# Operand addresses modulo 256: x, g and the sums moved by some tens of bytes in a pooled-attention and FFN kernel

## The chip, the core and the metric

The kernel runs on one NeuronCore of a Trainium2 chip; the other seven cores are idle. The metric is the device time of one execution in microseconds (us). The engines are named as in the profile: PE is TensorE (its weight loads, which overlap the matmuls, are PEld), DVE is VectorE, ACT is ScalarE, POOL is GpSimd, SP is the queue that issues the DMAs. Each engine runs its own instructions in order and waits on semaphores for the others. TensorE multiplies a *stationary* operand, loaded as weights, with a *streamed* operand that passes through it column by column. Both lie in SBUF, the on-chip memory of 128 partitions, where a tile is a range of bytes that has the same address in each partition. The text speaks of addresses *modulo 256*: the remainder of a tile's first byte when divided by 256.

## The reference

The inputs are q, k, v of shape 8 × 8 × 576 × 64 and the weights w_in (512 × 2048) and w_out (2048 × 512), all float32.

```python
k_p = k.reshape(B, H, Sp, 8, D).mean(axis=3)      # 576 keys pooled to 72
v_p = v.reshape(B, H, Sp, 8, D).mean(axis=3)
scores = scale * q @ k_p.T;  scores -= scores.max(-1)
attn = exp(scores) / (sum(exp(scores)) + 1e-9)
x = (attn @ v_p)  as 4608 tokens x 512
h = x @ w_in
g = max(h, 0) + log1p(exp(-abs(h)))               # softplus
out = g @ w_out                                    # 4608 x 512
```

## The kernel before

The 4,608 tokens are cut into 18 chunks of 256 (`CT`). Each chunk goes through attention, which leaves x for it, and then through the two products of the feed-forward part. The second axis of the weights is cut into 16 pieces of 128 (`FC`), treated in 8 pairs u (`FP`).

Each float32 operand of the large products is carried as a rounded high part and a low part, the remainder. A product is then three matmuls: high by high, high by low, low by high. In the first product (`ffn1_products`, L488) a 128 × 128 piece of w_in is stationary and 256 columns of x stream past it; a chunk has 16 × 4 × 3 = 192 such matmuls. Softplus on ACT gives g, a second activation its rounded part gh, and DVE the low part gl.

The second product exists in two forms. In the first four chunks (`ffn2`, L510, and `pair2`, L570) a 128-token piece of g is stationary and 512 columns of w_out stream. In the other fourteen (`pair2_fast`, L678) seven products of half width take the place of eight: sums and differences of g's quarters (`sums`, L588 to L591), rounded on ACT into `so` (L602) with a low part from DVE (L607), are stationary beside gh and gl, and 256 columns of w_out or of combined weights stream past them. That is 21 matmuls for each pair u.

The weights stay in SBUF: 16 tiles of 8,192 bytes per partition, in the pool `wpool`. All that comes and goes lies in the pool `one`: the loads (L, X4 to X6), q (A4), the pooled keys and values, the transposed q (G4, G5), the row minima mn and row sums sm of the softmax (two buffers of 32 bytes each), the exponentials E, the buffers G0 to G3, o0 and o1 for g, the sums and the outputs, pe for the normalized last eight columns, pT and Y for the transposed probabilities, X01 and X23 for x, and Sa and Sb for `so`. The x of the third chunk lies in Sa and Sb, before these hold sums.

Modulo 256 the kernel before has them so, with p for the place of the weights: q, the loads and qT at p; the minima and sums between p and p + 96; E at p + 32; buffer G3 at p + 128; everything behind pe (pT, x, the other buffers of g, gh, gl, so, the outputs) at p − 64. The tile pe has 192 floats in use and 16 more that nothing reads, 832 bytes in all.

The order of the work is computed ahead by a planner (`Order`): each operation has an engine, an estimated cost and its predecessors, and the planner lists them by rank and by hand-set offsets (`HASTE`). It knows slots (names of buffers), but no addresses. The program then issues every operation in that order, on all of ACT, DVE, PE and SP.

Of the kernel before, what the change touches and what calls it, by code (L numbers as in the profile page):

```python
# [9 lines left out]
F32 = mybir.dt.float32  # L10
F32R = mybir.dt.float32r
# [92 lines left out]
def pooled_attention_softplus_ffn(  # L104
# [11 lines left out]
    B, H, S, D = q.shape  # L116
    NTOK, DM = out.shape
    DFF = w_in.shape[1]
    P = 128
# [5 lines left out]
    CT = T * P  # L125
    HP = H // 2
# [3 lines left out]
    N1 = 3  # L130
# [5 lines left out]
    PSUM = bass.MemoryType.PSUM  # L136
    const = ctx.enter_context(tc.tile_pool(name="const", bufs=1))
    wpool = ctx.enter_context(tc.tile_pool(name="wpool", bufs=1))
    one = ctx.enter_context(tc.tile_pool(name="one", bufs=1))
    psum = ctx.enter_context(tc.tile_pool(name="psum", bufs=1, space=PSUM))  # L140
    dram = ctx.enter_context(tc.tile_pool(name="dram", bufs=1, space=bass.MemoryType.DRAM))
# [149 lines left out]
    R = 4 * KL  # L291
# [19 lines left out]
    def new_x(c, name=None):  # L311

        if c == N1 - 1:
            x_[c] = [one.tile([P, HP, CT], F32R, tag=tag, name="x") for tag in ("Sa", "Sb")]
        else:
            x = one.tile([P, 2, HP, CT], F32R, tag={"a": "X01", "b": "X23"}[name or "ab"[c % N1]],
                         name="x")
            x_[c] = [x[:, 0], x[:, 1]]

# [3 lines left out]
    class Tile:  # L323
# [30 lines left out]
        def least(self, j, ps, tag):  # L354

            if j == 0:
                self.mn = one.tile([P, 2, HP], F32, tag="mn" + tag, name="mn")
            nc.vector.tensor_reduce(out=self.mn[:, j], in_=self.view(ps), axis=AX.X, op=ALU.min)  # L358

        def view(self, ps):  # L360
# [9 lines left out]

        def exp_sum(self, j, ps, tag):
            if j == 0:
                self.sm = one.tile([P, H], F32, tag="sm" + tag, name="sm")
            for m in range(HP):
                h = 4 * (m // 2) + 2 * j + m % 2
                nc.scalar.activation(out=e_[self.c][:, self.t, h], in_=self.view(ps)[:, m],  # L376
                                     func=AF.Exp, scale=-1.0, bias=self.mn[:, j, m:m + 1],
                                     accum_out=self.sm[:, h:h + 1])

        def sum(self, tag):  # L380
            self.sm = one.tile([P, H], F32, tag="sm" + tag, name="sm")
            nc.vector.tensor_reduce(out=self.sm, in_=e_[self.c][:, self.t], axis=AX.X, op=ALU.add)

        def reciprocal(self):
# [7 lines left out]
                                    in1=self.sm.unsqueeze(2).to_broadcast([P, H, KM]), op=ALU.mult)  # L392

        def ends(self):

            pe = one.tile([P, 6 * R + 16], F32, tag="pe", name="pe")
            self.pe = pe[:, 0:6 * R].rearrange("p (a n r) -> p a n r", a=2, n=3)
            for a in range(2):
                hs = slice(4 * a, 4 * a + 4)
                nc.vector.tensor_tensor(  # L400
                    out=self.pe[:, a].rearrange("p n (h j) -> p n h j", h=4),
                    in0=e_[self.c][:, self.t, hs, KM:SP].unsqueeze(1).to_broadcast([P, 3, 4, KL]),
                    in1=self.sm[:, hs].unsqueeze(1).unsqueeze(3).to_broadcast([P, 3, 4, KL]),
                    op=ALU.mult)
# [61 lines left out]
    def av_high(c, r, ps, name=None):  # L466
        if c not in x_:
            new_x(c, name)
        nc.scalar.copy(out=x_[c][0][:, r::2], in_=ps.rearrange("p (g i) -> p g i", g=2))
# [475 lines left out]
    def attend(c):  # L945
# [17 lines left out]
        for t, x in enumerate(tiles):  # L963
# [7 lines left out]
            q_free[c, t] = o  # L971
            o = op(ACT, act(512), lambda x=x, s=s_q, n=s_qT: x.qT_out(s.tile, n.name), [o], [s_q, s_qT])
            ends, ss = [], [Slot("bank"), Slot("bank")]
            p = op(PE, 0.7, lambda x=x, ss=ss: x.scores([bank(s, "sc") for s in ss]), [o, *keys],
                   [s_qT, *ss])
            score_done.setdefault(c, []).append(p)
            for i, s in enumerate(ss):
                d = op(DVE, 0.46, lambda x=x, i=i, s=s, n=s_mn: x.least(i, s.tile, n.name), [p, *ends],
                       [s, s_mn])
                if c < N1:  # L980
                    def exp_sum(x=x, i=i, s=s, e=s_E[0], t=t, n=s_sm):
                        if c == 0 and 0 not in e_:
                            new_E(0)
                        e_[c] = e_[0]
                        x.slot = e.name
                        x.exp_sum(i, s.tile, n.name)
                    ends.append(op(ACT, 1.2, exp_sum, [d], [s, s_mn, s_sm, *s_E], table="exp"))
                else:
                    def less(x=x, i=i, s=s):
                        if c not in e_:  # L990
                            new_E(c)
                        x.less(i, s.tile)
                    ends.append(op(DVE, 0.46, less, [d, *e_free], [s, s_mn]))
            if c < N1:
                exps.extend(ends)
            else:
                subs += ends
            norms.append((x, ends, s_E, s_sm, s_pm, s_pe))
        if c == N1:
            ex = op(ACT, 1.2, lambda: exponential(e_[c]), subs, table="exp")  # L1000
# [403 lines left out]
```

## Time and profile before

| | us |
|---|---|
| two runs | 903.52 and 904.15, median 903.84 |
| the profiled execution | 903.13 |
| its span on the core | 901.4 |
| PE busy | 883.9 (98%) |
| PEld busy | 840.9 (93%) |
| DVE busy | 648.7 (72%) |
| ACT busy | 407.5 (45%) |
| DMA queue q1 | 189.82 MB, 68.2% of 16 engines |

A group of the profile names line, engine and operation, the output and its inputs by the program's names, the shape, the count, busy time in us and the mean of one in ns, and the engine's idle time ahead of them with what ended it. Matmuls overlap in the pipeline: one lasts some 280 ns from its start to its end, but the next starts far earlier, so their throughput is read from the distance between starts. The timeline merges equal neighbours into one row with the start of the first, the time to the end of the last, and the count. The chain is the sequence of work that ended last, followed back from the last instruction. In the rows by windows stand, for each engine, busy time and number of instructions, then the granted clock, the share of the DMA engines and GB/s.

### The profile page before, as it was taken

Reading aid. Unit: us, or ns where it says so; the run is one execution under the profiler, and the core shown is the slowest. Engines: PE = TensorE matmul, PEld = TensorE weight load, DVE = VectorE, ACT = ScalarE, POOL = GpSimd, SP = SyncE. Lnnn points to the kernel's source line nnn. Section 1 sums busy time; section 2 is a strip of 40 time slices with the busy share of each in tenths; the row PEclk is TensorE's granted clock in tenths of the full one; section 3 lists DMA queues with packets and bytes.
Section 4 is the critical chain, followed back from the end, with each engine's and each line's share of the span. In section 5 each row is a group of like instructions: output and inputs, shape, how many; then the busy total and the mean of one; then the engine's idle time right before and its main releaser. Section 6 shows DMA issues by size and latency. Waiting matters only on the chain.

```text
span 901.4 us, 20496 instructions
## 1 busy us (share of the span) xinstructions
PE 883.9 (98%) x8304; PEld 840.9 (93%) x8304; DVE 648.7 (72%) x1600; ACT 407.5 (45%) x824; POOL 2.4 (0%) x19
## 2 busy tenths in 40 slices
PE   5999999999999999999999999999999999999997
PEld 3689999889999999999999999999999999999997
DVE  5899999878767678787767666776576565657454
ACT  5864443354353534443444444353545353434332
POOL 1000000000000000000000000000000000000000
PEclk9999999999999999999999999999999999999999
DMA  9976544545997788787669765877566565656472
GB/s 233 312 227 202 173 162 158 161 153 200 299 267 240 231 239 245 214 249 228 227 200 261 217 227 168 257 239 228 193 179 228 177 222 187 212 162 225 163 241 76
DMA packets 107085, 191.12 MB, mean 212 GB/s; under 512 B 46064, under 2 KB 60400, under 8 KB 106992
## 3 DMA queue, kind: packets, MB, share of 16 engines
q1 hardware_dynamic: 106992, 189.82, 68.2%
q8 instruction: 65, 1.06, 0.5%
q14 instruction: 28, 0.23, 0.1%
HBM read 167.25 MB, written 22.54 MB: 211 GB/s over the span
## 4 chain that ended last, share of the span: by engine, by line
PE 95%; DVE 2%; DMA 1%; SPq 1%; ACT 1%; issue 0%; DVEq 0%; ACTq 0%
PE h L488 44%; PE m L678 31%; PE acc L510 7%; PE acc L570 3%; PE sc L351 2%; PE avp L455 2%; PE qTp L331 2%; PE ptp L414 2%; PE avp L462 1%; DMA wst<-in_moe_w_out_dram 1%; PE ltp L426 1%; DMA kvl<-in_v_dram 1%; ACT E L376 0%; SPq L302 0%; DVE o L699 0%
## 5 line engine op out<-in xcount | busy, mean ns | idle before, releaser
L488 PE MATMUL h<-x,w 128*128 128x256 f32 x3456 | 428.7, 280 | 0.2 <-ACT g L493 0.2
L488 PEld LDWEIGHTS h<-x,w 128*128 128x128 f32 x3456 | 413.3, 188 | 4.2 <-ACT g L493 0.6
L537 ACT ACTIVATE g<-h 128x512 f32<-128x512 f32 x120 | 71.9, 599 | 280.3 <-PE h L488 277.7
L678 PE MATMUL m<-w,so 128*128 128x256 f32 x1344 | 173.9, 278 | 0.0
L678 PEld LDWEIGHTS m<-w,so 128*128 128x128 f32 x1344 | 163.8, 188 | 0.0
L678 PE MATMUL m<-w,gh 128*128 128x256 f32 x672 | 131.6, 285 | 0.0
L588 DVE TENSOR_TENSOR sf<-g 128x128 f32<-128x128 f32 x112 | 32.7, 292 | 130.1 <-ACT g L537 129.6
L678 PEld LDWEIGHTS m<-w,gh 128*128 128x128 f32 x672 | 102.1, 188 | 1.7
L602 ACT CAST so<-sf 128x512 fp32r<-128x512 f32 x112 | 69.7, 622 | 58.1 <-DVE sf L591 57.6
L607 DVE TENSOR_TENSOR so<-sf,so 128x512 fp32r<-128x512 f32 x112 | 77.3, 690 | 22.8 <-ACT so L602 22.7
L678 PE MATMUL m<-w,gl 128*128 128x256 f32 x336 | 93.5, 278 | 0.0
L558 DVE TENSOR_TENSOR gl<-g,gh 128x384 fp32r<-128x384 f32 (+1 forms) x120 | 67.2, 560 | 0.5 <-ACT gh L551 0.3
L678 PEld LDWEIGHTS m<-w,gl 128*128 128x128 f32 x336 | 63.0, 188 | 0.0
L510 PE MATMUL acc<-w,g 128*128 128x512 f32 x192 | 60.1, 394 | 0.0
L551 ACT ACTIVATE gh<-h 128x384 fp32r<-128x384 f32 (+1 forms) x120 | 59.2, 493 | 0.0
L493 ACT ACTIVATE g<-h 128x256 fp32r<-128x256 f32 x96 | 32.1, 383 | 56.6 <-PE h L488 34.3
L699 DVE TENSOR_TENSOR o<-o,m 128x256 f32<-128x256 f32 x98 | 39.7, 417 | 3.5 <-ACT o L691 0.6
L510 PEld LDWEIGHTS acc<-w,g 128*128 128x128 f32 x192 | 33.5, 188 | 5.2
L510 PE MATMUL acc<-w,gl 128*128 128x512 f32 x96 | 37.9, 395 | 0.2 <-DVE gl L499 0.2
L591 DVE TENSOR_TENSOR sf<-g,sf 128x128 f32<-128x128 f32 x112 | 32.7, 292 | 3.9
L358 DVE TENSOR_REDUCE mn<-sc 128x4 f32<-128x288 f32 x72 | 31.3, 450 | 5.5 <-PE sc L351 5.4
L400 DVE TENSOR_TENSOR pe<-E,sm 128x96 f32<-128x96 f32 x72 | 15.2, 252 | 27.7 <-PE ltp L426 27.7
(165 smaller groups left out, 925.8 us busy)
## 6 DMA issues: line engine op xcount, KB each, us to landing
w<-wi SPq DMA_DIRECT2D x224, 512.0 KB
out_dram<-o SPq DMA_DIRECT2D x36, 256.0 KB
q<-in_q_dram SPq DMA_DIRECT2D x32, 256.0 KB
wst<-in_moe_w_in_dram SPq DMA_DIRECT2D x32, 256.0 KB
wst<-in_moe_w_out_dram SPq DMA_DIRECT2D x16, 512.0 KB
wi<-w SPq DMA_DIRECT2D x16, 512.0 KB
kst<-in_k_dram SPq DMA_DIRECT2D x24, 288.0 KB
vst<-in_v_dram SPq DMA_DIRECT2D x24, 256.0 KB
```

What stands on the lines that cost most here:

```text
L488: nc.tensor.matmul(out=ps[:, 0:CT], lhsT=row(w, kc), rhs=x[:, kc], start=first and kc == j == 0, stop=last and kc == KC - 1 and j == 2)
L493: nc.scalar.activation(out=g, in_=ps[:, 0:CT], func=AF.Softplus)
L510: nc.tensor.matmul(out=accs[c][t], lhsT=a[:, ts], rhs=w, start=f == 0 and j == 0, stop=f == FC - 1 and j == 2)
L537: nc.scalar.activation(out=g, in_=x.rearrange("p (b i) -> p b i", i=P), func=AF.Softplus)
L551: nc.scalar.activation(out=gh, in_=quarters(c, x.rearrange("p (b i) -> p b i", i=P)), func=AF.Softplus)
L558: nc.vector.tensor_tensor(out=gl, in0=quarters(c, g), in1=gh.bitcast(F32), op=ALU.subtract)
L588: tt(out=sf[:, 2], in0=g[:, 0], in1=g[:, 2], op=ALU.add)
L591: tt(out=sf[:, 3], in0=g[:, 3], in1=sf[:, 1], op=ALU.subtract)
L602: nc.scalar.copy(out=so[:, 0], in_=ss[c, u])
L607: nc.vector.tensor_tensor(out=so[:, 1], in0=sf, in1=so[:, 0].bitcast(F32), op=ALU.subtract)
L678: nc.tensor.matmul(out=ms[c][n], lhsT=x, rhs=y, start=u == 0 and j == 0 and n in (1, 6, 5, 4), stop=u == FP - 1 and j == 2 and n in (2, 7, ...
L699: nc.vector.tensor_tensor(out=o, in0=in0, in1=m[n], op=how)
```

## The change

The tiles of x for all chunks but the third leave the big pool for one of their own, which opens behind an unused tile of 32 bytes; the minima and sums get a small pool with an unused tile of 64 bytes; and pe loses its 16 unused floats. Operations, their order, their shapes and the number of buffers stay.

```diff
     wpool = ctx.enter_context(tc.tile_pool(name="wpool", bufs=1))
+    room = ctx.enter_context(tc.tile_pool(name="room", bufs=1))
+    room.tile([P, 8], F32, name="room")
+    xpool = ctx.enter_context(tc.tile_pool(name="xpool", bufs=1))
+    mpool = ctx.enter_context(tc.tile_pool(name="mpool", bufs=1))
+    mpool.tile([P, 16], F32, name="room")
     one = ctx.enter_context(tc.tile_pool(name="one", bufs=1))
...
-            x = one.tile([P, 2, HP, CT], F32R, tag={"a": "X01", "b": "X23"}[name or "ab"[c % N1]],
+            x = xpool.tile([P, 2, HP, CT], F32R, tag={"a": "X01", "b": "X23"}[name or "ab"[c % N1]],
                          name="x")
...
-                self.mn = one.tile([P, 2, HP], F32, tag="mn" + tag, name="mn")
+                self.mn = mpool.tile([P, 2, HP], F32, tag="mn" + tag, name="mn")
...
-                self.sm = one.tile([P, H], F32, tag="sm" + tag, name="sm")
+                self.sm = mpool.tile([P, H], F32, tag="sm" + tag, name="sm")
...
         def sum(self, tag):
-            self.sm = one.tile([P, H], F32, tag="sm" + tag, name="sm")
+            self.sm = mpool.tile([P, H], F32, tag="sm" + tag, name="sm")
...
         def ends(self):
-
-            pe = one.tile([P, 6 * R + 16], F32, tag="pe", name="pe")
-            self.pe = pe[:, 0:6 * R].rearrange("p (a n r) -> p a n r", a=2, n=3)
+            self.pe = one.tile([P, 2, 3, R], F32, tag="pe", name="pe")
```

## The prediction

> **What bounds the kernel now.** I read the page's engine table and chain first, to see which engine sets the end and with which lines; then the groups of its two large lines; then the timeline of TensorE alone in the middle of the run, because the change alters no instruction and can only act through how long one of them takes.
>
> ```profile
> span 901.4 us, 20496 instructions
> ...
> PE 883.9 (98%) x8304; PEld 840.9 (93%) x8304; DVE 648.7 (72%) x1600; ACT 407.5 (45%) x824; POOL 2.4 (0%) x19
> ...
> PEclk9999999999999999999999999999999999999999
> ...
> PE 95%; DVE 2%; DMA 1%; SPq 1%; ACT 1%; issue 0%; DVEq 0%; ACTq 0%
> PE h L488 44%; PE m L678 31%; PE acc L510 7%; PE acc L570 3%; PE sc L351 2%; PE avp L455 2%; PE qTp L331 2%; PE ptp L414 2%; PE avp L462 1%; DMA wst<-in_moe_w_out_dram 1%; PE ltp L426 1%; DMA kvl<-in_v_dram 1%; ACT E L376 0%; SPq L302 0%; DVE o L699 0%
> ```
>
> TensorE is 98% busy at full clock and is 95% of the chain. Nothing off TensorE can give back more than a few per cent, and 75% of the chain is two lines: L488 (the first product, x streams past a stationary piece of w) and L678 (the fast second product, w streams past a stationary piece of g or of a sum).
>
> ```profile
> L488 PE MATMUL h<-x,w 128*128 128x256 f32 x3456 | 428.7, 280 | 0.2 <-ACT g L493 0.2
> ...
> L678 PE MATMUL m<-w,so 128*128 128x256 f32 x1344 | 173.9, 278 | 0.0
> ...
> L678 PE MATMUL m<-w,gh 128*128 128x256 f32 x672 | 131.6, 285 | 0.0
> ...
> L678 PE MATMUL m<-w,gl 128*128 128x256 f32 x336 | 93.5, 278 | 0.0
> ```
>
> That is 3,456 of L488 and 1,344 + 672 + 336 = 2,352 of L678, 5,808 matmuls of one shape. Their idle time is nil, so what counts is how far apart they start. The timeline merges equal neighbours (start, time from first start to last end, count), and it shows two speeds for the same work:
>
> ```profile
> 489.52 2.90 PE L488 MATMUL h<-x,w 128*128 128x256 f32 x24
> ...
> 492.94 1.52 PE L678 MATMUL m<-w,so 128*128 128x256 f32 x12
> 494.30 0.39 PE L678 MATMUL m<-w,gh 128*128 128x256 f32 x2
> 494.52 0.28 PE L678 MATMUL m<-w,gl 128*128 128x256 f32 x1
> 494.64 2.99 PE L488 MATMUL h<-x,w 128*128 128x256 f32 x24
> ...
> 498.18 1.57 PE L678 MATMUL m<-w,so 128*128 128x256 f32 x12
> 499.59 0.40 PE L678 MATMUL m<-w,gh 128*128 128x256 f32 x2
> 499.83 0.28 PE L678 MATMUL m<-w,gl 128*128 128x256 f32 x1
> 499.94 0.60 PE L414 MATMUL ptp<-ident,pm 128*128 128x128 f32 x4
> ```
>
> One matmul alone lasts 0.28 us, so twelve that take 1.52 start (1.52 − 0.28)/11 = 113 ns apart, and twelve that take 1.57 start 117 ns apart. Counted by starts the two spacings are 113.3 and 117.8 ns, and hardly anything lies between them: a group falls into one and stays in it to its end. Engine, shape, clock and operands' places modulo 256 are the same in both. The pass of 45 matmuls from 489.52 to 494.64 takes 5.12 us, the next, from 494.64 to 499.94, takes 5.30. So the kernel alternates between a fast and a slow gait, and which one it has depends on how it started, not on which data it reads.
>
> How often each? Of the 112 groups of twelve on the sums, 110 stand unbroken in the timeline; 47 take 1.52 and 63 take 1.57 to 1.61. First and last of them:
>
> ```profile
> 244.60 1.52 PE L678 MATMUL m<-w,so 128*128 128x256 f32 x12
> ...
> 894.65 1.61 PE L678 MATMUL m<-w,so 128*128 128x256 f32 x12
> ```
>
> So 57% of L678 is slow. For L488 the length of a group also holds a wait at its start, so I counted the starts themselves: of its 3,366 spacings between 112 and 130 ns, 1,600 are 116 or more (48%), mean 115.59. For L678 there are 2,303 such spacings, mean 115.94.
>
> **The change, by its addresses.** Let p be the weights' place modulo 256 (all 16 weight tiles are 8,192 B, so they share it). Before, the tiles ahead of x and g in the big pool are multiples of 256 B except two minima and two sums of 32 B and pe, which is 832 B = 3×256 + 64. So x, g, gh, gl, so stand at p + 4×32 + 64 = p − 64 modulo 256 (the buffer G3, ahead of pe, at p + 128). After, room (32 B) puts x at p + 32; the two x tiles are 8,192 B each, the small pool holds 64 + 4×32 = 192 B, so the big pool begins at p + 32 + 192 = p − 32, and as pe is now 768 B, all of it stands there. In terms of what TensorE reads, the streamed operand against the stationary one: L488 goes from −64 to +32, L678, L510 and L570 from +64 to +32. The x of the third chunk lies in the sums' buffers, so the 192 matmuls of L488 that read it go to −32.
>
> No instruction, wait, queue or transfer is added, removed or moved; the order on each engine comes from a planner that knows no addresses. Net space is +32 B. So the sum has one kind of term: so many matmuls by the change of their spacing.
>
> *Why the place can matter at all.* The streamed operand covers 256×4 = 1,024 B of each partition per matmul, the weights loaded meanwhile for the next 128×4 = 512 B. Modulo 256 the first laps the second twice per matmul. If a meeting costs some 4.5 ns, one meeting and two give two spacings 4.5 ns apart, as seen. Where both operands are 128 wide there is nothing to lap, and the transposes bear that out:
>
> ```profile
> L414 PEld LDWEIGHTS ptp<-ident,pm x144: 138/140/144, 22.2 to 834.2; 128*128 128x128 f32 x144
> L414 PE MATMUL ptp<-ident,pm x144: 270/272/328, 22.3 to 834.3; 128*128 128x128 f32 x144
> ```
>
> Four of them take 0.60 us (row above), so they start (0.60 − 0.27)/3 = 110 ns apart (109 by starts), as pm lies at either of two places. By this reading 109 is no meeting, 113.3 one, 117.8 two. It is an inference, not a row.
>
> *What +32 does.* If the stream starts 32 B ahead of the weights it has to gain 224 B to the first meeting and 480 of 512 to the second, which then falls at 94% of the matmul; by their starts the next weights set out 2 to 5 ns after the stream, so it may fall past the end. From +64 the second is at 448, from −64 at 320. So +32 should prefer one meeting, the fast gait, in both large lines, and I take 113.3 ns throughout. The bounds are 109 (no meeting) and 117.8 (always two); one step further is 122.3 (three).
>
> *Terms.* L488: 3,366 × (115.59 − 113.33) = 7.6 us. L678: 2,303 × (115.94 − 113.33) = 6.0 us. The early second products stream 512 columns:
>
> ```profile
> L510 PE MATMUL acc<-w,g 128*128 128x512 f32 x192 | 60.1, 394 | 0.0
> ...
> 152.53 0.62 PE L510 MATMUL acc<-w,g 128*128 128x512 f32 x2
> 152.98 0.39 PE L510 MATMUL acc<-w,gl 128*128 128x512 f32 x1
> 153.21 0.62 PE L510 MATMUL acc<-w,g 128*128 128x512 f32 x2
> ```
>
> Three take 153.21 − 152.53 = 0.68 us, about 229 each; single starts are 226, 229 and 232 apart. Their 366 spacings have mean 229.8; at 226 they give 1.4 us, at 232 they cost 0.8. Sum: 7.6 + 6.0 + 1.4 = 15.0 us. The profiled execution took 903.1 us (span 901.4 and 1.7 around it), so 903.1 − 15.0 = **888 us**. That execution is 0.7 below the median of the runs shown, 903.84; I keep 888.
>
> *Other engines.* DVE and ACT move too. A multiply on DVE shows that places matter there as well:
>
> ```profile
> L391 DVE TENSOR_TENSOR pm<-E,sm x36: 639/684/693, 20.7 to 831.3; 128x512 f32<-128x512 f32 x36
> ...
> 350.00:450.00 100.00, 100.00 (x980) 97.88 (x978) 74.97 (x204) 45.89 (x82) 0.00 (x0) 1.00 0.76 228
> ```
>
> Same shape, 639 to 693 ns; at worst 36 × 54 ns = 1.9 us of DVE, at best the same the other way. I take nothing, because between 350 and 450 us DVE is 75% and ACT 46% busy (third and fourth busy figures) while TensorE is full; without that cover it would cost the 1.9 us. Transposes, scores and attention products keep their time: the transposes do not react to pm's place, and the 96 products of L462 are worth at most 96 × 4.5 ns = 0.4 us.
>
> TensorE has two reads at once here. The Trainium skill (TensorE: Matmul & The Clock Gate, Part 2, step 1) says that the weight load and the streamed operand have independent read ports, and that loading does not take bandwidth from the running matmul. By that rule the sum would be 0 instead of 15.0. The two gaits of one shape do not settle this, but they show that something between two matmuls costs time.
>
> **Rivals.**
>
> *Places mean nothing to TensorE* (0.22). The two gaits are then a property of the start alone, say of how the weight queue runs ahead, and come out in the same mixture: 903, or 895 to 908 if the mixture shifts. For it: the streamed operand of L488 is 64 B behind, that of L678 64 B ahead, and both have the same two spacings. Against it: L414 with equal widths has none. The skill's rule above is this case.
>
> *No meeting at all* (0.17). At 109 ns: L488 saves 3,366 × 6.4 = 21.5 us, L678 2,303 × 6.7 = 15.5 us, with 1.4 from the wide ones 38.4: 865. It needs the second lap to vanish and the first to cost nothing. Against it: not one steady group of 256 columns runs at 109 in this trace. Half of the way is possible (865 to 884). The Trainium skill (TensorE: Matmul & The Clock Gate, Back-to-back issue gap) gives an isolated gap of N/2.4 + 2.5 ns, which for 256 columns is 109.2; no run here shows it at that width.
>
> *The slow gait everywhere* (0.16). If meetings are as likely from +32 as from ±64 but closer to the hand-over to the next matmul, each pass ends with a meeting and starts with the next: two for all. It costs 3,366 × (117.8 − 115.59) + 2,303 × (117.8 − 115.94) + 0.8 = 7.4 + 4.3 + 0.8 = 12.5 us: 916. It decides from about half: if more than the present 48% and 57% are slow, the change loses. A third meeting (122.3 ns) would give +37 us, 940; I give that 0.06 of the 0.16. For it: 57% of L678 is already slow at +64, the nearest place to +32.
>
> *The forecast* has the other 0.45, spread over 884 to 892.
>
> That the new pools are laid otherwise than I work out is within the first rival; all sizes are fixed, so I give it no price of its own.
>
> **The numbers.** The likeliest case gives 888. The range reaches from 868, most of the way to the no-meeting case, to 910, past the no-effect case; what is left out is some 0.04 below and 0.14 above. Faster by over 2% means under 885.8 us, slower by over 2% above 921.9; 2% is about what a measurement of this kernel can tell from no change. Under 885.8: the 0.17 of the no-meeting case and a fifth of the forecast, 0.26. Over 921.9: the third meeting and a little, 0.07. The rest, 0.67, is within.
>
> **What would show it.** In the timeline after, groups of twelve on the sums at 1.52 throughout and groups of 24 of L488 at 2.90 (2.98 with a wait at the start) confirm the step. A remaining mixture of 1.52 and 1.57 near 43 to 57 says that the place is nothing; 1.57 throughout is the slow case; 1.48 or less ((109×11 + 276) ns) is no meeting. L488 and L678 can differ: they had opposite signs before and have one now, and the third chunk's L488, at −32, is a contrast inside the run. I am wrong if the time moves while these spacings do not, or if DVE or a transfer appears in the chain with more than its present 2% and 1%.

## The result, and the profile after

The changed kernel takes 912.1 us (median of 911.8 and 912.4) where the kernel before takes 903.8: a ratio of 1.0086, with a 95% interval of 1.0063 to 1.0108. It is slower by about 8 us; the forecast was faster by 15. It lies inside the 2% that were named as no change, and outside the range of 868 to 910.

The page of the changed kernel, in the same parts as before (lines are shifted: L492 is the former L488, L682 the former L678, L514 the former L510):

```profile
span 910.1 us, 20496 instructions
...
PE 893.6 (98%) x8304; PEld 849.0 (93%) x8304; DVE 649.3 (71%) x1600; ACT 407.4 (45%) x824; POOL 2.4 (0%) x19
...
PE 96%; DVE 1%; DMA 1%; ACT 1%; issue 0%; SPq 0%; DVEq 0%; ACTq 0%
...
L492 PE MATMUL h<-x,w 128*128 128x256 f32 x3456 | 434.1, 281 | 0.0
...
L682 PE MATMUL m<-w,so 128*128 128x256 f32 x1344 | 175.3, 279 | 0.0
```

PE has grown by 9.7 us, DVE by 0.6, and ACT not at all; the counts are the same. TensorE still has no idle time ahead of these lines. So the time went into the matmuls themselves, and the timeline of TensorE (start, time to the end of the last, count) shows how:

```profile
449.98 1.56 PE L682 MATMUL m<-w,so 128*128 128x256 f32 x12
451.38 0.40 PE L682 MATMUL m<-w,gh 128*128 128x256 f32 x2
451.62 0.28 PE L682 MATMUL m<-w,gl 128*128 128x256 f32 x1
451.74 2.98 PE L492 MATMUL h<-x,w 128*128 128x256 f32 x24
...
456.04 1.56 PE L682 MATMUL m<-w,so 128*128 128x256 f32 x12
```

Twelve matmuls on the sums took 1.52 or 1.57 us before. Now they take 1.56: of the 107 groups that stand unbroken in the timeline, 85 take 1.56 and none less. Neither of the two old gaits is left. By single starts, which the trace has in whole ns, the spacings now run in a circle, for instance 113, 116, 117, 120 and again 113: mean 116.7 ns. Others run 116, 118, 119, mean 117.8.

From start to start, summed over each line: first product 407.9 to 413.3 us (+5.4), fast second product 277.1 to 279.9 (+2.8), the wide matmuls of the early second products, with 512 columns, 90.5 to 91.2 (+0.7). That is 8.9 us, against 8.7 of the span; all else together changed by 0.2. In the table "mean" is that of all spacings from 112 to 130 ns (222 to 245 for the wide ones), "fast" the share of 115 ns or less. That share counts single spacings, and a circle such as 113, 116, 117, 120 has short ones too. Counted by groups that nothing interrupts, 44 of 85 of the first product and 35 of 65 of the second ended at a steady 113.3 before, and none of the same 85 and 65 does now.

| kernel | us | first: mean, fast | second: mean, fast | wide: mean |
|---|---|---|---|---|
| before | 903.8 | 115.59, 52% | 115.94, 43% | 229.8 |
| changed | 912.1 | 117.19, 16% | 117.18, 18% | 232.3 |

### The profile page after: what moved, and what is told of

It is laid out like the page before. It is cut to its first block, busy times and chain, and to the rows that moved or that the text cites. A ratio compares the mean times of both kernels' runs of the same rounds, so it can differ in the third digit from the quotient of the medians.

```text
span 910.1 us, 20496 instructions
## 1 busy us (share of the span) xinstructions
PE 893.6 (98%) x8304; PEld 849.0 (93%) x8304; DVE 649.3 (71%) x1600; ACT 407.4 (45%) x824; POOL 2.4 (0%) x19
## 4 chain that ended last, share of the span: by engine, by line
PE 96%; DVE 1%; DMA 1%; ACT 1%; issue 0%; SPq 0%; DVEq 0%; ACTq 0%
PE h L492 44%; PE m L682 31%; PE acc L514 7%; PE acc L574 3%; PE sc L357 2%; PE avp L459 2%; PE qTp L337 2%; PE ptp L418 2%; PE avp L466 1%; PE ltp L430 1%; PE kps L920 1%; DMA kvl<-in_v_dram 1%; DMA kvst<-in_k_dram 0%; ACT E L382 0%; PE kvlp L879 0%; DVE o L703 0%
## 5 line engine op out<-in xcount | busy, mean ns | idle before, releaser
L492 PE MATMUL h<-x,w 128*128 128x256 f32 x3456 | 434.1, 281 | 0.0
L492 PEld LDWEIGHTS h<-x,w 128*128 128x128 f32 x3456 | 418.4, 188 | 4.1 <-ACT g L497 0.4
L682 PE MATMUL m<-w,so 128*128 128x256 f32 x1344 | 175.3, 279 | 0.0
L682 PEld LDWEIGHTS m<-w,so 128*128 128x128 f32 x1344 | 165.2, 188 | 0.0
L682 PE MATMUL m<-w,gh 128*128 128x256 f32 x672 | 132.7, 286 | 0.0
L682 PEld LDWEIGHTS m<-w,gh 128*128 128x128 f32 x672 | 102.2, 188 | 1.7
L682 PE MATMUL m<-w,gl 128*128 128x256 f32 x336 | 94.2, 280 | 0.0
L682 PEld LDWEIGHTS m<-w,gl 128*128 128x128 f32 x336 | 63.2, 188 | 0.0
L514 PE MATMUL acc<-w,g 128*128 128x512 f32 x192 | 60.7, 397 | 0.0
L514 PEld LDWEIGHTS acc<-w,g 128*128 128x128 f32 x192 | 33.6, 188 | 5.4
L514 PE MATMUL acc<-w,gl 128*128 128x512 f32 x96 | 37.9, 395 | 0.2 <-DVE gl L503 0.2
```

The lines of the kernel that those rows point to most:

```text
L492: nc.tensor.matmul(out=ps[:, 0:CT], lhsT=row(w, kc), rhs=x[:, kc], start=first and kc == j == 0, stop=last and kc == KC - 1 and j == 2)
L514: nc.tensor.matmul(out=accs[c][t], lhsT=a[:, ts], rhs=w, start=f == 0 and j == 0, stop=f == FC - 1 and j == 2)
L682: nc.tensor.matmul(out=ms[c][n], lhsT=x, rhs=y, start=u == 0 and j == 0 and n in (1, 6, 5, 4), stop=u == FP - 1 and j == 2 and n in (2, 7, ...
```

## The experiments

A place is given as a number of bytes ahead of the weights, modulo 256: before, x and g (with gl and the sums) are at 192 (that is −64); in the changed kernel x is at 32 and g at 224 (−32). The distance of the streamed operand from the stationary one is x's place in the first product and 256 less g's place in the second. The theories: **A**, the distance modulo 256 sets the spacing; **B**, besides, one product hands its gait to the next; **C**, it is the other engines; **D**, distances count only modulo 64. Each timed run has the kernel before beside it on the same chip. The diffs are shortened, with remarks behind #; in those of the matmuls alone, words stand for the loops.

### The matmuls alone

A kernel of its own: no attention, no softplus, no real output; a narrower matmul ahead of each group of 24.

```diff
+ for n in (64, 96, 128, 160, 192, 224):     # six starts
+     one matmul of n columns
+     24 matmuls: (hi, xh), (lo, xh), (hi, xl) over four pieces, x shifted by a floats
+ # for a = 0, 4, ... 60 (0 to 240 B), then six cases with both operands moved
```

> Matmuls alone: one stationary and one streamed tile (rounded float32, 128 x 128 against 256 columns), 24 in a group in the order of L488 (high by high, low by high, high by low), six groups for each distance of the two operands from 0 to 240 B in steps of 16, each group behind one narrower matmul that shifts its start; then six cases in which both operands are moved together. No other engine works meanwhile, and attention, weights and output are left out. If the distance modulo 256 sets the spacing (theory A), 64 and 192 show 113.3 ns or 117.8 by group, 32 shows orbits between 113 and 120 with a mean of 116.7 to 117.8, and a pair moved together keeps what its distance had. If the spacing in the kernel comes from the other engines (theory C), all distances give one spacing here. If distance counts only modulo 64 (theory D), 0, 64, 128 and 192 look alike, and 32, 96, 160 and 224 too.

Groups by form of that run, each 144 matmuls of one distance (L49 is 16 B, L51 32, L55 64, L59 96, L71 192; L79 and L83 are 192 with both operands moved by 64 and by 128 B):

```profile
L49 PE MATMUL h<-x,w 128*128 128x256 f32 x144 | 17.3, 279 | 0.0
L51 PE MATMUL h<-x,w 128*128 128x256 f32 x144 | 17.6, 281 | 0.0
L55 PE MATMUL h<-x,w 128*128 128x256 f32 x144 | 17.8, 281 | 0.0
L59 PE MATMUL h<-x,w 128*128 128x256 f32 x144 | 18.1, 284 | 0.0
L71 PE MATMUL h<-x,w 128*128 128x256 f32 x144 | 17.5, 281 | 0.0
...
L79 PE MATMUL h<-x,w 128*128 128x256 f32 x144 | 17.6, 281 | 0.0
...
L83 PE MATMUL h<-x,w 128*128 128x256 f32 x144 | 17.6, 281 | 0.0
```

Nothing but the place differs, and no other engine is at work, yet 144 matmuls take 17.3 to 18.1 us. By starts, the mean of the last 18 of a group's 23 spacings (the program's very first group, at 0 B, began at 213 ns and is left out):

| distance, B | spacing, ns | distance, B | spacing, ns |
|---|---|---|---|
| 0 | 119.6 (120.0 at the end) | 128 | 118.4 to 120.0 |
| 16 | 113.3 (one start 118.7) | 144 | 118.4 to 119.0 |
| 32 | 116.4 to 117.8 | 160 | 117.4 to 120.0 |
| 48 | 118.4 | 176 | 119.3 |
| 64 | 117.8 | 192 | 113.3 or 117.8 |
| 80 | 118.1 to 120.1 | 208 | 119.2 |
| 96 | 120.0 | 224 | 118.3 |
| 112 | 115.1 to 115.9 (113.3 at the end, from all six starts) | 240 | 116.9 to 117.4 |

The numbers of the kernels come out on the spot: 192, which the first product had before, has both old gaits; 32 has the new ones. Moving both operands together changes nothing: all three cases at 192 have 113.3 or 117.8 again, all three at 32 have 116.4 to 117.8. So C falls, and D too (0, 64, 128 and 192 differ). A holds so far, with one limit: at several places the start chooses among gaits. The run has distances from 0 to 240 B, with pieces of 512 B; that the period is 256 B was not tried by itself.

### x alone and the big pool alone

```diff
  # e2: x at 32, all else at 192          # e3: x at 192, all else at 224
- mpool.tile([P, 16], F32, name="room")
+ gap.tile([P, 8], F32, name="gap")       # e3: the small pool first, then 64 B, x, 32 B
```

> x at p + 32 as in the changed kernel, the big pool at p - 64 as before. Theory A: L488 takes the changed kernel's spacings (mean 117.2 below 130 ns, +5.4 us), the second products those of before (115.9): 903.8 + 5.4 = 909. Theory C (the big pool's place against the weights slows the other engines or their writes): 904. If one product hands its gait to the next (theory B), L678 changes too although its operands stand as before, and the time is not the sum.

> x at p - 64 as before, the big pool at p - 32 as in the changed kernel. Theory A: L488 as before (115.6), the second products as in the changed kernel (117.1, and 232 for the wide ones): +2.3 and +0.9, 907. Theory C: 912. Theory B: L488 changes too, and e2 and e3 do not add up to 912.

| kernel | us | first: mean, fast | second: mean, fast | wide: mean |
|---|---|---|---|---|
| e2, x alone | 913.6, ratio 1.0102 (1.0086 to 1.0117) | 117.04, 19% | 117.49, 8% | 230.3 |
| e3, big pool alone | 907.4, ratio 1.0032 (1.0018 to 1.0046) | 115.29, 59% | 116.97, 20% | 232.9 |

Each part alone costs time, and x alone as much as the whole change: from start to start, summed over the three kinds of matmul, 8.8 us in e2, 3.1 in e3 and 8.9 for both together. By A alone 909 and 907 were forecast. The reason for the miss in e2 is in its second product: its operands stand as in the kernel before, and yet it fell from 43% fast to 8%. The first product no longer arrives in the fast gait, and at its distance of 64 the second finds the slow one. This fits B on top of A: the parts do not add up (9.6 + 3.4 us against 8.3 by the medians, 8.8 + 3.1 against 8.9 in the matmuls). Some 2 us of e2's profiled execution lie outside these lines: its first 50 us hold 411 matmuls at a granted clock of 0.93, those of before 451 at 1.00. I have not followed that, and so do not count the 1.5 us by which e2's median lies above that of the whole change.

### Distance 0 and distance 64

```diff
  # e4: x and the big pool at 0           # e7: x at 64, big pool at 192
- room.tile([P, 8], F32, name="room")
+ room.tile([P, 16], F32, name="room")    # e7; in e4 no room here and 128 B ahead of the big pool
```

> x and the big pool at p, so all distances between stream and stationary operand are 0. Theory A with my lapping picture: meetings at 0, 256 and 512 B of gain, so two to three, 117.8 to 122 ns, 916 to 940. Theory D (only modulo 64 counts): as before with its 64, 904.

> L488 at +64 in place of -64, everything else with the distances of before. Measured alone, 64 gave 117.8 ns from every start, 192 gave 113.3 or 117.8. Theory A: L488 rises to 117.8, 3,366 x 2.2 = +7.4. With handing over (theory B) the second products lose the fast starts that L488 gave them: 2,303 x (117.8 - 115.9) = +4.3 more: 916. Without it 911. If only the size of the distance counts: 904.

At distance 0 the kernel takes 927.4 us (ratio 1.0252, 1.0234 to 1.0270), within the 916 to 940 that the lapping picture gave; both products run at 119.8 ns, near the 119.6 of the matmuls alone. At 64 it takes 914.0 (ratio 1.0097, 1.0079 to 1.0115): the first product at 117.4 with 9% fast, and the second, with its operands untouched, at 117.7 with 1% fast. The groups of twelve in e7's timeline:

```profile
494.12 1.57 PE L681 MATMUL m<-w,so 128*128 128x256 f32 x12
...
495.88 2.99 PE L491 MATMUL h<-x,w 128*128 128x256 f32 x24
```

Of 109 such groups on the sums that stand unbroken 108 take 1.57 or more (47 had 1.52 before). Both numbers were forecast from the run of matmuls alone and from handing over (916 with it, 911 without, 904 if only the size of the distance counted).

### 16 B ahead in both products

This is the place at which the matmuls alone held 113.3 ns from nearly every start and almost at once; at 112 B all six starts get there too, but only after 10 to 13 spacings. As pools place tiles on multiples of 32 B, the x buffers become slices of one tile, and so do those of gh, gl and so; a second kernel has the same slices at the old places.

```diff
- x = xpool.tile([P, 2, HP, CT], F32R, tag=..., name="x")
+ x = xall[:, i:i + 2 * HP * CT].rearrange("p (h m i) -> p h m i", h=2, m=HP)   # i starts at 16 B
- so = one.tile([P, 2, 4, P], F32R, tag="S" + tag, name="so")
+ so = piece("S" + tag, 8 * P).rearrange("p (h b i) -> p h b i", h=2, b=4)
```

> The stream 16 B ahead of the stationary operand in both large products: x at p + 16, the buffers of gh, gl and so at p - 16 (each set of buffers is now one tile cut into slices, as the pools place tiles on multiples of 32 B); the third chunk's x is at p - 16. Theory A with the spacings measured alone (113.3 ns at 16 B from every start but one, 116.9 at 240): L488 saves 3,366 x (115.59 - 113.33) = 7.6 less 192 x 3.6 ns = 0.7, the second products 6.0, the wide ones unknown within 1.4: 904 - 13 = 891. If the gait in the kernel is set by other engines and not by the distance: 904 to 912.

> The same slices as in the run with 16 B, but with x, gh, gl and so at p - 64 as before: it tells the effect of the places from that of cutting one tile into slices. Theory A: spacings and time as before, 904. If the slices change waits and these count: as far from 904 as the run with 16 B.

With the slices at the old places the time is that of before (904.6, ratio 1.0000, 0.9987 to 1.0013; 115.63 and 116.02 ns). With 16 B it is 914.6 (ratio 1.0104, 1.0081 to 1.0126), neither 891 nor within the 904 to 912 of the other case. The first product holds 113.3 in many groups (39% fast), but in others it runs 117, 118, 121, 117, 120 (mean 118.5) or 114, 119 in turn; mean 116.66. The second has 12% fast, mean 118.37. So A and B as I had put them do not suffice: one distance has more gaits than my six starts had found, and the second product, in which the stationary operand is repeated (gh, gh, gl) where in the first the stream is (xh, xh, xl), has other gaits at the same distance.

### Widths, and steps of 4 B

Matmuls alone again, the loop as above with the stationary operand of m and the stream of n columns.

```diff
- nc.tensor.matmul(out=h[:, 0:n], lhsT=y, rhs=z, start=s, stop=e)
+ nc.tensor.matmul(out=h[0:m, 0:n], lhsT=y, rhs=z, start=s, stop=e)
```

> Matmuls alone as in the first such run, now with the stream 4, 8, 12, 20, 24 and 28 B ahead at 256 columns, and at 0, 16, 32, 64 B (and 192 for the first) with 512 columns, with a stationary operand of 64 columns, and with 128 columns on both sides. Lapping picture (the stream overtakes the load of the next weights, each meeting costs 4 to 5 ns): half the load means half the meetings, so 64 columns give at most 113.3 at all distances and 109 at the best; 128 against 128 columns at full rate have one lap too, so 113.3 or 109 and not more. If the extra time is a hand-over between matmuls that only starts at certain times, 64 columns change nothing. Within 4 to 28 B I expect 113.3 around 16 and a step to 116 or more on both sides; no number for where.

| case | spacing, ns |
|---|---|
| 4 B; 8; 12; 20; 24; 28 B ahead, 128 against 256 | 122 to 123; 116.7 or 126.7; 116.7; 122.2; 120.0; 115.6 |
| stationary 64 columns, stream 256: 0; 16; 32; 64 B | 113.3 to 120.0; 113.3 to 117.8; 117.7 to 119.2; 113.3 to 116.7 |
| 128 against 128: 0; 16; 32; 64 B | 111.5 to 111.9 at all four |
| 128 against 512: 0; 16; 32; 64; 192 B | 226.7; 231.8; 233.2; 229.0; 233.4 |

Half the stationary columns do not halve the extra time: the spacings are 113.3 at the least and up to 120, as with 128 columns, where the picture of meetings allowed 113.3 at the most. That speaks against the picture that I forecast with. The order of the places is another, though: with 64 columns 0 B has 113.3 from five of six starts. The fast place at 16 B is narrow: 12 and 20 B give 116.7 and 122.2. With 128 columns on both sides place counts for nothing at the four distances tried. And the wide matmuls have their own order: 226.7 at 0, where 256 columns are at their slowest.

### Pairs of places

```diff
+ for a, b in 256 pairs of places:      # x a floats, g b floats ahead of the weights
+     twice: 24 matmuls as of L488, then 21 as of L678
```

> Matmuls alone in the two orders of the kernel, 24 as of L488 and 21 as of L678 in turn, twice for each of 256 pairs of places: x 0 to 240 B ahead of the weights and g 0 to 240 B ahead, in steps of 16. No attention between, no waits, no other engine. If distance and handing over (theories A and B together) are all there is, a pass at the places of before (192 and 192) runs at 113.3 or 117.8 and a pass at the changed kernel's (32 and 224) at 116.7 to 117.8, as in the kernels between their attention parts; the second product's spacing at one g depends on where x is. Without handing over it doesn't: one number for each g, whatever x. Some pair may hold 113.3 in both products, and that would be the one to try in the kernel.

In the timeline of this run, L97 has x at 16 and g at 64, L129 x at 32 and g at 64:

```profile
230.41 2.56 PE L97 MATMUL m<-w,g 128*128 128x256 f32 x21
...
235.61 2.56 PE L97 MATMUL m<-w,g 128*128 128x256 f32 x21
...
399.67 2.64 PE L129 MATMUL m<-w,g 128*128 128x256 f32 x21
...
404.98 2.64 PE L129 MATMUL m<-w,g 128*128 128x256 f32 x21
```

The rows are the second product with the same places of g and w. After a first product at x = 16 its 21 matmuls take 2.56 us (113.3 ns settled), after one at x = 32 2.64 (117.8). This is handing over with no other engine in the program. Over all pairs, the first product held 113.3 for some or all g at x = 16, 64, 112, 144 and 192, the second at g = 64 and 192. In no pass did both hold 113.3. The changed kernel's pair (32 and 224) had 117.8 in both products in its first pass and 116.7 in both in its second; the pair of before (192 and 192) had 117.8 in both products and both passes. By this run alone the change would have cost nothing. So the lead of the kernel before seems to come from the starts that it gives: in the first run of matmuls alone, 192 had 113.3 from some starts and 117.8 from others, and in the kernel about half of the groups find the first.

### Three pairs and a fourth in the kernel

```diff
  # the slices of e5, at other places:
  # e10: x 144, g 224    e11: x 192, g 64    e12: x 16, g 64    e14: x 112, g 64
```

> x at p + 144, gh, gl and so at p - 32 (224), in slices: the pair with the shortest pass when measured alone (113.3 for the first product, 116.7 for the second). If what was measured alone carries over: L488 saves 7.6 less 0.7 for the third chunk's x at 224, the second products cost 2,303 x 0.75 ns = 1.7, the wide ones 1.3 (233.2 against 229.8 ns): 904 - 4 = 900. If the attention parts between the passes choose other gaits, as in the run with 16 B: up to 912.

> x at p - 64 as before, gh, gl and so at p + 64, so that the stream stands 64 B behind in both products. Measured alone this pair had 113.5 and 117.8, but at g = 64 the second product held 113.3 from six of sixteen starts, at g = 192 from three. By the pair alone: L488 -7.0, second products +4.3, wide ones unknown within 1.4: 901. If the gait depends on the starts that the kernel gives: anywhere from 891 (all fast) to 916 (all slow), below 904 if g = 64 is entered more easily.

> x at p + 16, gh, gl and so at p + 64. Measured alone: 116.5 and 113.3. L488 +3.1 us, the second products -6.0: 901 if it carries over; the run with 16 B in both products gave L488 116.6 in the kernel, so this part should hold. If the second products find the slow gait: 904 + 3 + 4 = 911.

> x at p + 112, gh, gl and so at p + 64. Measured alone 112 gave 113.3 to 116.7 from all starts (mean 115.2), and g = 64 held 81% at 113 to 115 in the kernel with x at 16. If a place brings its gait along whatever the start: L488 115.2 (-1.3), second products 114.4 (-3.5), wide ones +1.4: 900. If the gaits depend on what the kernel hands over, as at 144 (where 113.3 was often seen alone and 118.1 in the kernel): 904 to 916.

| kernel | us | ratio (95%) | first: mean, fast | second: mean, fast | wide |
|---|---|---|---|---|---|
| e10 | 916.8 | 1.0137 (1.0122 to 1.0152) | 118.12, 13% | 117.14, 14% | 232.8 |
| e11 | 906.7 | 1.0033 (1.0020 to 1.0046) | 115.65, 51% | 116.39, 34% | 232.2 |
| e12 | 907.0 | 1.0036 (1.0024 to 1.0048) | 117.03, 38% | 114.38, 81% | 233.3 |
| e14 | 909.6 | 1.0051 (1.0033 to 1.0068) | 116.07, 50% | 116.41, 34% | 232.6 |

Alone, the first product at 144 with g at 224 had 118.8 in one pass and 113.3 in the other; in the kernel it has 118.1, and e10 came out above both of its forecasts. The second product at 64 behind x = 16 carried over:

```profile
496.10 2.56 PE L695 MATMUL m<-w,g 128*128 128x256 f32 x21
498.50 2.96 PE L505 MATMUL h<-x,w 128*128 128x256 f32 x24
501.30 2.56 PE L695 MATMUL m<-w,g 128*128 128x256 f32 x21
```

In e12 the second product is 1.6 ns faster than before, 81% of it in the fast gait, but the first product gives back 1.4 ns on half as many matmuls again, and the wide ones 3.5; 907.0 lies between the two forecasts, 901 and 911. In e14 the same g has 34%: again the product ahead decides, and alone this pair had 117.8 in the second product as well. The first product of e14 carried over too, but late: all of its 81 groups of 24 that nothing interrupts run at 113.3 from the 15th spacing on, and at most 41% of them do before that, so the place pays only in the last 9 of 23 spacings. None of these beats the kernel before.

### Own weights or the next ones

```diff
+ # two stationary operands in turn, the second 32 B further on
+ # cases 1 to 5: each stream D ahead of its own; cases 6 to 10: D ahead of the next one
```

> Matmuls alone with two stationary operands in turn, the second's place 32 B further on. In the first five cases each stream stands D = 0, 16, 32, 64, 192 B ahead of its own stationary operand (so 32 less and 32 more than D against the next one); in the last five D ahead of the next one (32 more and 32 less against its own). If the stream and the load of the next weights are what meets, the last five give the spacings that one distance gave alone: 120, 113.3, 116.7, 117.8, and 113.3 or 117.8, and the first five don't. If it is the stream and its own weights, the first five do. If neither does, the order of streams or of loads among themselves counts too.

Neither half repeats the table. With D = 0, 16, 32, 64, 192 against the stream's own weights the groups settle at 116.8 to 118.9, 116.7, 116.5 to 117.7, 117.7 to 119.9 and 119.1 to 120.4 ns; against the next weights at 116.8 to 118.6, 116.4 to 116.8, 118.7 to 119.0, 116.4 to 118.0 and 118.4 to 120.3. So the spacing is not a matter of one distance alone; what it is in two or three successive matmuls that delays them stays open.

## Why the prediction was wrong, point by point

**What bounds the kernel** was read rightly: all of the 8.7 us is in the distance between the starts of the matmuls, and nothing of it in waits, DVE or transfers.

**The addresses** are as worked out, and that the other engines would not show is right as well (DVE +0.6 us of busy time, behind a full TensorE). The multiply of L391 turned out to be no sign that places matter there: it takes the same 639 to 695 ns, in the same order, before, after and in e2 and e4, in which the sums stand at other distances from the exponentials.

**"So +32 should prefer one meeting, the fast gait"** is the step that failed. At 32 B there is no steady 113.3 at all: alone it has 116.4 to 117.8, and in the changed kernel 16% and 18% of the spacings are at 115 or less, where 52% and 43% were, and these are the short steps of circles: no uninterrupted group ends at 113.3. The two terms came out at +5.4 in place of −7.6 and at +2.8 in place of −6.0; the wide term at +0.7 in place of −1.4, inside its bounds.

**The picture behind it**, a stream that laps the load of the next weights, was called an inference, and it fell on three counts. First, the places at which the first product most often held 113.3 among the pairs, 112 and 192 (29 and 26 of 32 passes), put the second meeting at 400 and 320 of the 512 bytes that the stream gains; at 32 and 48, which put it at 480 and 464, none of 64 passes held it. Second, with half the stationary columns the spacings still reach 120. Third, the distance to the next weights alone does not set the spacing. I had fitted one free idea to two numbers, 113.3 and 117.8, and then let it choose between places that the trace of before did not contain.

**The bounds** were wrong at the top and idle at the bottom. For 128 against 256 columns no steady group ran below 113.3 in any run, so the 109 of the transposes was no bound for this shape; upward, distance 0 has 119.8, and steps of 4 B reach 126.7, where I stopped at 117.8 or 122.3.

**The rivals.** That places mean nothing is refuted by the matmuls alone: 144 of them take 17.3 or 18.1 us by the place of their operands. The Trainium skill (TensorE: Matmul & The Clock Gate, Part 2, step 1) says that loading the next weights takes no read bandwidth from the running matmul. I had read from it that places would change nothing, and that reading does not hold here; whether it is the load that delays the matmuls, no run shows. The slow case had the right sign and gave 916, near the measured 912, and its condition (more than 48% and 57% slow) came true; its mechanism, two meetings at 117.8 everywhere, did not: the new gaits are others.

**The sum** took the two products as independent, although the first part of the prediction had said that a group's gait depends on how it started. With x alone moved the second product lost its fast gait too, and the matmuls lost as much as by the whole change. This term, the handing over, was missing; in e2 it is 2,303 × 1.55 ns = 3.6 us, about half of each of the two large terms.

What stays open: by what the matmuls delay each other, and so how to work out the gaits of a place in advance.

## What to carry to other kernels

Where TensorE is full, look at the spacing of equal matmuls in the timeline before anything else: two spacings for one shape mean that something outside the program's logic has a say, and here operand addresses modulo 256 moved this kernel between 904 and 927 us with not one instruction changed. Any edit that shifts tiles by some tens of bytes (a pad, a new small tile, another pool) can do this, so compare spacings before you credit or blame the edit itself. The picture chose wrongly, and matmuls measured alone were half a guide: the second product of e12 and the first of e14 came out as alone, the pair of before did not. So a place has to be tried in the kernel, and both products together, because each hands its gait to the next. Look also at how many spacings a group needs until it is steady: 14 of 23, as in e14, eat up most of what a good place saves.

## What the runs showed of the hardware that I had not expected

Streams of identical rounded float32 matmuls settle into circles of fixed length: 113.3 ns for each, or 116.7 in circles of four (113, 116, 117, 120), or 117.8, 118.5, 120.0, up to 126.7 (at 8 B), by the operands' places and by the start. 128 against 128 columns have 111.5 to 111.9 ns at all four distances tried. And with 512 columns the order of places is another (226.7 at 0 B, 233.2 at 32), so one pad that helps the one shape can cost the other: the wide matmuls lost 3.5 ns each in e12, while the second product gained 1.6.
